# Moving one transposing load of x from SyncE's DMA queue to ScalarE's in a fused linear-attention kernel

## The chip, the cores and the metric

The kernel runs on one core of a Trainium2 chip. The metric is the device time of one execution in microseconds (us); a time that is quoted for a kernel is the median of its runs. A profile comes from one execution, and its span runs from the first to the last instruction that it recorded.

## The reference

Two linear-attention blocks, A and B, read the same x (A_x; B_x is not used), and a per-token gate mixes their outputs. S = 2048 tokens, D = 640 features, H = 32 heads of 20 features, everything in bf16.

```
def block(x, wqkv, wo):                       # once with A's weights, once with B's
    q, k, v = split(x @ wqkv)                 # 32 heads of 20
    phi = lambda t: where(t > 0, t + 1, exp(t)) + 1e-6
    pq, pk = phi(q), phi(k)
    kv = einsum("bhsd,bhse->bhde", pk, v)
    z  = einsum("bhsd->bhd", pk)
    num = einsum("bhqd,bhde->bhqe", pq, kv)
    den = einsum("bhqd,bhd->bhq", pq, z)[..., None] + 1e-6
    return (num / den).reshape(B, S, D) @ wo
g = sigmoid((x * gate_w).sum(-1, keepdims=True))
out = g * block(x, A_wqkv, A_wo) + (1 - g) * block(x, B_wqkv, B_wo)
```

## The kernel before

The tokens are cut into 16 tiles of 128 (NT). The work comes in four stages, one after the other on TensorE.

**Stage k.** For every token tile t and for X = A, B, `k_unit(X, t)` multiplies the tile of x^T by the k part of the weights. There are five steps (`k_step`, over NC = 5 chunks of 128 features); each is a 128x512 and a 128x128 matmul (129 columns for B, whose last column holds the gate), at lines 502 and 503. ScalarE takes the exponential (line 535) and VectorE finishes phi (lines 538 and 546). For tiles 0 and 1 the order is written out by hand: A for both tiles, chunk by chunk, then B for both tiles. From tile 2 on it is tile by tile, A and then B. So tile 2 is 20 matmuls, tile 3 the next 20, and so on.

**Stage g.** `g_unit` sums phi(k)^T x over all tokens (lines 632 and 633), with `q_unit` (line 755) between. **Then** `kv_unit` (673), `wp_unit` (709, 710) and the denominators (838) build one 640x640 matrix W' for each block, and **the last stage** (`o_mm`, line 925) multiplies phi(q) by W' and writes the output.

**Loads.** The matmuls of stage k need x transposed (buffer XT, features on partitions). For tiles 0 and 1, x is loaded as it stands (into XN) and TensorE transposes it against an identity (`x_tp`, line 449), after which VectorE copies it to XT (line 464). For tiles 2 to 15 the DMA transposes while it loads: `xt_dma(t0, t1)` issues one transposing DMA for tiles t0 to t1 - 1. Before the change, all of these come from SyncE's queue (called SP in the profile). SP's loads are issued in the order in which the program lists them:

- x of tile 0, A's k weights chunk 0, x of tile 1, A's k weights chunks 1 to 4 (wkA0 to wkA4)
- B's k weights chunks 0 to 4 (wkB0 to wkB4)
- the seven transposing loads: tile 2, 3, 4, 5, 6 and 7, 8 to 11, 12 to 15 (called xt2, xt3, xt4, xt5, xt6, xt8, xt12 here)
- x of tiles 2 to 15 as it stands, then WQ, WV and WO of both blocks

ScalarE's queue (ACT) issues two small loads at the start: the constants (CST, with the identity) and the gate weights (GW). Then it loads its table with a dummy exponential (line 380), and has nothing more until the first exponentials of stage k.

**Who sets the order.** A small list scheduler (`Sched`) places every operation by estimated costs. TensorE's order is the program's; on the other engines it takes what is ready first. While loads are being listed, each load is tied behind the one before it on the same queue (`o.behind = chain.get(q)`). A dependency between engines, or on a DMA, becomes a semaphore wait ahead of the waiting instruction, and what follows on that engine stands behind it. `after` adds such dependencies by hand. All DMAs are issued at line 349.

Of the kernel before, what the change touches and what calls it, by code (L numbers as in the profile page):

```python
# [6 lines left out]
ACT = mybir.ActivationFunctionType  # L7
# [252 lines left out]
def body(nc, A_x, A_wqkv, A_wo, B_x, B_wqkv, B_wo, gate_w, out, log=None):  # L260
# [84 lines left out]
    def dma(q, name, dst, src, nbytes, ins=(), outs=(), after=(), issue=450.0, transpose=False, prio=None):  # L345
        def fn(e):
            d = dst() if callable(dst) else dst
            with nc.allow_non_contiguous_dma(reason="layout"):
                return e.dma_start(d, src() if callable(src) else src, transpose=transpose)  # L349

        o = op(q, fn, 0.0, ins, outs, after, prio=prio, name=name, dma=(issue, nbytes, 95.0 if transpose else 330.0))
        if loading:
            o.behind = chain.get(q)
            chain[q] = o
        return o
# [14 lines left out]
    bxn = [Buf("xn%d" % t) for t in range(NT)]  # L370
    bxt = [Buf("xt%d" % t) for t in range(NT)]
# [15 lines left out]
    def ld_wk(q, X, c, after=()):  # L387
        dma(q, "wk%s%d" % (X, c), WK[X][:, c, 0:D], wqkv[X][128 * c : 128 * c + 128, D : 2 * D], 163840, outs=[bwk[X, c]], after=after)

    def xt_dma(t0, t1):  # L390
        dma(
            "SP",
            "xt%d" % t0,
            XT[:, :, 128 * t0 : 128 * t1],
            x[128 * t0 : 128 * t1, :],
            (t1 - t0) * 163840,
            outs=bxt[t0:t1],
            issue=(t1 - t0) * 850.0,
            transpose=True,
        )  # L400

    def w3(X, k):
# [8 lines left out]
        ld_wk("SP", "A", c)  # L411
    for c in range(NC):
        ld_wk("SP", "B", c)
    for t0, t1 in ((2, 3), (3, 4), (4, 5), (5, 6), (6, 8), (8, 12), (12, 16)):
        xt_dma(t0, t1)
    dma("SP", "xr", XN[:, 2:NT, 0:D], x[256:S, :].rearrange("(t p) d -> p t d", p=128), 14 * 163840, outs=bxn[2:])
    for X in XS:
# [655 lines left out]
def bass_gated_mix__linear_attn_block__linear_attn_block__prompt_kernel(nc, *args):  # L1073
    body(nc, *args)
# [28 lines left out]
```

## Time and profile before

| | |
|---|---|
| three runs | 189.91, 190.32, 190.47 us; median 190.32 |
| profiled execution | 190.32 us; its span is 189.0 us |
| granted TensorE clock | 1.000 over the span |
| TensorE matmul (PE) | 184.9 us busy, 98% of the span |
| VectorE (DVE), ScalarE (ACT) | 128.6 us (68%), 95.9 us (51%) |
| DMA | 19.42 MB |

How to read the profile: PE is TensorE's matmul and PEld its weight load, which overlaps the matmuls before it. SPq and ACTq are what the sequencers of SyncE and ScalarE spend on issuing DMAs. A DMA is issued at one time and lands later; "us to landing" is the time between, counted from the start of the issue. The chain of waits is followed back from the last instruction, at each step to what released it. A weight load that starts right behind the previous one shows that TensorE waited for nothing there.

### The profile page before, as it was taken

What the parts mean: (1) busy time and instruction counts of PE and PEld (TensorE: products, weight loads), DVE (VectorE), ACT (ScalarE), POOL (GpSimd) and SP (SyncE); (2) the same over time, 40 slices, a digit from 0 to 9 for tenths busy, and PEclk for the clock granted to TensorE, in tenths of its full rate; (3) what the DMA queues carried; (4) which work ended last, traced back from release to release, by engine and by line L of the source; (5) the groups of instructions that cost most, each with busy time, mean ns of one, the idle gap of its engine ahead of it and who ended that gap; (6) DMA issues with size and microseconds to landing.
All of it is one profiled execution on the core that took longest, in us unless ns stands there. A gap on an engine that the chain in (4) does not pass through costs nothing.

```text
span 189.0 us, 3188 instructions
## 1 busy us (share of the span) xinstructions
PE 184.9 (98%) x1246; PEld 108.3 (57%) x1270; DVE 128.6 (68%) x252; ACT 95.9 (51%) x172; POOL 0.3 (0%) x6
## 2 busy tenths in 40 slices
PE   8999999999999999999999999999999999999995
PEld 3555555555565656656557556655666655555552
DVE  2389888888833556477787698888996962765600
ACT  3255565656554545544584777877626495100012
POOL 0000000000000000000000000000000000000000
PEclk9999999999999999999999999999999999999999
DMA  6999999996014011012000006340011055133322
GB/s 194 283 157 141 242 393 365 356 222 139 3 43 106 0 38 35 0 35 30 8 16 18 3 0 147 104 104 5 0 40 30 17 142 129 38 137 107 136 75 69
DMA packets 29469, 19.42 MB, mean 103 GB/s; under 512 B 17390, under 2 KB 29198, under 8 KB 29454
## 3 DMA queue, kind: packets, MB, share of 16 engines
q1 hardware_dynamic: 29300, 19.17, 39.4%
q8 instruction: 10, 0.16, 0.4%
q10 hardware_dynamic: 154, 0.05, 0.1%
q14 instruction: 5, 0.04, 0.1%
HBM read 9.95 MB, written 2.64 MB: 67 GB/s over the span
## 4 chain that ended last, share of the span: by engine, by line
PE 96%; DMA 2%; issue 1%; SPq 0%; DVE 0%; DVEq 0%
PE ps L925 23%; PE ps L755 22%; PE ps L632 18%; PE ps L502 18%; PE ps L503 5%; PE ps L633 5%; DMA XN<-in_A_x_dram 2%; PE ps L673 2%; PE ps L709 1%; SPq L349 0%; PE ps L449 0%; PE ps L710 0%; PE ps L838 0%; DVE TSB L969 0%; PE ps L483 0%
## 5 line engine op out<-in xcount | busy, mean ns | idle before, releaser
L502 PE MATMUL ps<-WKW,XT 128*128 128x512 bf16 x154 | 43.6, 384 | 0.1
L772 ACT ACTIVATE EK<-ps 128x512 bf16<-128x512 f32 x40 | 23.9, 599 | 31.3 <-PE ps L755 30.1
L503 PE MATMUL ps<-WKW,XT 128*128 128x128 bf16 (+1 forms) x160 | 35.3, 221 | 0.3
L535 ACT ACTIVATE EK<-ps 128x640 bf16<-128x640 f32 x32 | 22.3, 703 | 12.8 <-PE ps L503 8.6
L502 PEld LDWEIGHTS ps<-WKW,XT 128*128 128x128 bf16 x160 | 15.8, 99 | 19.1 <-DVE XT L464 0.6
L755 PE MATMUL ps<-XT,WQA 128*128 128x512 bf16 x96 | 24.0, 379 | 0.1
L755 PE MATMUL ps<-XT,WQB 128*128 128x512 bf16 x95 | 23.3, 379 | 0.4 <-issue 0.2
L632 PE MATMUL ps<-XN,PKB 128*128 128x512 bf16 x80 | 23.5, 379 | 0.0
L782 DVE TENSOR_SCALAR EK<-EK 128x512 bf16<-128x512 bf16 x40 | 11.6, 290 | 17.5 <-ACT EK L772 17.4
L632 PE MATMUL ps<-XN,PKA 128*128 128x512 bf16 x78 | 23.1, 379 | 0.1
L633 PE MATMUL ps<-XN,PKA 128*128 128x129 bf16 x80 | 17.6, 220 | 0.1
L633 PE MATMUL ps<-XN,PKB 128*128 128x129 bf16 x80 | 17.6, 220 | 0.0
L925 PE MATMUL ps<-WPA,EX 128*128 128x128 bf16 (+1 forms) x117 | 17.0, 297 | 0.2
L925 PE MATMUL ps<-WPB,PKA 128*128 128x128 bf16 (+1 forms) x117 | 16.1, 297 | 0.2
L503 PEld LDWEIGHTS ps<-WKW,XT 128*128 128x128 bf16 x160 | 15.8, 99 | 0.0
L755 PEld LDWEIGHTS ps<-XT,WQB 128*128 128x128 bf16 x100 | 10.9, 118 | 8.5 <-issue 0.2
L755 PEld LDWEIGHTS ps<-XT,WQA 128*128 128x128 bf16 x100 | 10.6, 117 | 8.1
L538 DVE TENSOR_SCALAR EK<-EK 128x640 bf16<-128x640 bf16 x32 | 10.4, 325 | 7.0 <-ACT EK L535 7.0
L632 PEld LDWEIGHTS ps<-XN,PKA 128*128 128x128 bf16 x80 | 9.4, 117 | 7.9
L632 PEld LDWEIGHTS ps<-XN,PKB 128*128 128x128 bf16 x80 | 9.4, 117 | 7.8
L971 ACT ACTIVATE TSB<-ps 128x640 bf16<-128x640 f32 (+1 forms) x3 | 2.0, 668 | 23.2 <-PE ps L925 23.2
L546 DVE SCALAR_TENSOR_TENSOR PKA<-ps,EK 128x640 bf16<-128x640 f32 x16 | 13.2, 825 | 0.6
(78 smaller groups left out, 233.1 us busy)
## 6 DMA issues: line engine op xcount, KB each, us to landing
out_dram<-TSB SPq DMA_DIRECT2D x15, 160.0 KB, 1.8
XN<-in_A_x_dram SPq DMA_DIRECT2D x1, 2240.0 KB, 8.8
WKW<-in_A_wqkv_dram SPq DMA_DIRECT2D x5, 160.0 KB, 3.4
WKW<-in_B_wqkv_dram SPq DMA_DIRECT2D x5, 160.0 KB, 4.1
WQA<-in_A_wqkv_dram SPq DMA_DIRECT2D x1, 800.0 KB, 10.5
WQB<-in_B_wqkv_dram SPq DMA_DIRECT2D x1, 800.0 KB, 11.7
WVA<-in_A_wqkv_dram SPq DMA_DIRECT2D x1, 800.0 KB, 12.8
WVB<-in_B_wqkv_dram SPq DMA_DIRECT2D x1, 800.0 KB, 14.1
```

The costliest lines, as they stand in the source:

```text
L502: e.matmul(a[:, 0:512], l, WK[X][:, c, 0:512], start=(c == 0), stop=(c == NC - 1))
L503: return e.matmul(a[:, 512:w], l, WK[X][:, c, 512:w], start=(c == 0), stop=(c == NC - 1))
L535: op("ACT", lambda e: e.activation(EK[:, ek.slot, :], psw(ps, D), ACT.Exp), act_cost(D), ins=[ps] + first, outs=[ek], name="ke")
L538: lambda e: e.tensor_scalar(EK[:, ek.slot, :], EK[:, ek.slot, :], 1.0, EPS, op0=ALU.min, op1=ALU.add),
L546: lambda e: e.scalar_tensor_tensor(PKt[X][:, t, :], psw(ps, D), 0.0, EK[:, ek.slot, :], op0=ALU.max, op1=ALU.add),
L632: e.matmul(a[:, 0:512], l, XN[:, t, 0:512], start=(t == 0), stop=(t == NT - 1))
L633: return e.matmul(a[:, 512 : D + 1], l, XN[:, t, 512 : D + 1], start=(t == 0), stop=(t == NT - 1))
L673: r = e.matmul(PS[0:GR, ps.slot, GR * i : GR * i + GR], WV[X][:, c, lo : lo + GR], gv[:, c, :, lo // 5 : lo // 5 + 24], start=(c == 0), st ...
L755: r = e.matmul(PS[:, ps.slot, :], WQ[X][:, c, g::5], XT[:, c, 512 * b : 512 * b + 512], start=(c == 0), stop=(c == NC - 1),)
L772: lambda e: e.activation(EQ[:, eq.slot, :], PS[:, ps.slot, :], ACT.Exp),
L782: lambda e: e.tensor_scalar(EQ[:, eq.slot, :], EQ[:, eq.slot, :], 1.0, EPS, op0=ALU.min, op1=ALU.add),
L925: r = e.matmul(a[:, l0 - lo : h0 - lo], PQ[X, b][:, g, 128 * (t % 4) : 128 * (t % 4) + 128], WP[X][:, g, l0:h0], start=(X == first and g = ...
```

## The change

`xt_dma` takes a queue and a list of things to wait for. The load of tile 2 (xt2) goes to ScalarE's queue and waits until x of tile 1 has landed (`bxn[1].writers` is that DMA). The load of tile 3 (xt3) stays on SP and waits until xt2 has landed (`bxt[2].writers` is the DMA of xt2). The other five transposing loads, and all loads behind them on SP, follow xt3 as before.

```diff
-    def xt_dma(t0, t1):
+    def xt_dma(t0, t1, q="SP", after=()):
         dma(
-            "SP",
+            q,
             "xt%d" % t0,
             XT[:, :, 128 * t0 : 128 * t1],
             x[128 * t0 : 128 * t1, :],
...
             issue=(t1 - t0) * 850.0,
             transpose=True,
+            after=after,
         )
...
-    for t0, t1 in ((2, 3), (3, 4), (4, 5), (5, 6), (6, 8), (8, 12), (12, 16)):
+    xt_dma(2, 3, "ACT", bxn[1].writers)
+    xt_dma(3, 4, "SP", bxt[2].writers)
+    for t0, t1 in ( (4, 5), (5, 6), (6, 8), (8, 12), (12, 16)):
         xt_dma(t0, t1)
```

The order of the instructions on TensorE, VectorE and GpSimd is the same in both programs. On ScalarE, xt2 stands between the dummy exponential and the first exponential of stage k. On SP the first transposing load, now xt3, carries the wait for xt2.

## The prediction

> **What bounds the kernel now.** First the engines on the page, then the chain of waits on the page.
>
> ```profile
> PE 184.9 (98%) x1246; PEld 108.3 (57%) x1270; DVE 128.6 (68%) x252; ACT 95.9 (51%) x172; POOL 0.3 (0%) x6
> PE 96%; DMA 2%; issue 1%; SPq 0%; DVE 0%; DVEq 0%
> ```
>
> TensorE is busy for 98% of the span, and 96% of the chain is TensorE. The only DMA on the chain is one load of x. The chain of waits of the first 14 us shows it:
>
> ```profile
> 0.91 3.55 DMA XN<-in_A_x_dram
> 4.51 0.72 PE ps L449 x5
> ```
>
> It is x of tile 1, issued at 0.91 and landed at 0.91 + 3.55 = 4.46. From there on the chain is TensorE. So a change to the loads can take time from the kernel only where TensorE waits for a load, and can add time only by making it wait; a wait early in stage k moves all that follows by its own length, since TensorE has no idle time later to absorb it.
>
> Next the timeline of TensorE around the first matmuls that use a transposing load. These are weight loads; columns are start, duration, engine, line.
>
> ```profile
> 10.84 0.10 PEld L502 LDWEIGHTS ps<-WKW,XT 128*128 128x128 bf16 x1
> ...
> 13.56 0.10 PEld L502 LDWEIGHTS ps<-WKW,XT 128*128 128x128 bf16 x1
> ```
>
> Tile 2 starts at 10.84, tile 3 at 13.56, so one tile takes 2.72 us, and the weight loads come at their usual step of 0.27 us: no wait at either. Tile 4 is due at 13.56 + 2.72 = 16.28, tile 5 at 19.00, tile 6 at 21.72, tile 8 at 27.16, tile 12 at 38.04.
>
> Then SP's timeline and, by narrow windows of the DMA view, the time from issue to landing of each transposing load (the last column). xt2, xt3, xt4, xt5 in that order, then the one for GSA, which the kernel issues much later, at 58.04, from SBUF and beside little else:
>
> ```profile
> 5.66 14.46 SPq L349 DMA_TRANSPOSE XT<-in_A_x_dram  x7
> ```
>
> ```profile
> XT<-in_A_x_dram SPq DMA_TRANSPOSE x1, 4.5
> ```
>
> ```profile
> XT<-in_A_x_dram SPq DMA_TRANSPOSE x1, 3.8
> ```
>
> ```profile
> XT<-in_A_x_dram SPq DMA_TRANSPOSE x1, 3.9
> ```
>
> ```profile
> XT<-in_A_x_dram SPq DMA_TRANSPOSE x1, 4.0
> ```
>
> ```profile
> GSA<-WKW SPq DMA_TRANSPOSE x1, 2.6
> ```
>
> xt2 lands at 5.66 + 4.5 = 10.2, which is 0.7 ahead of its use. xt3 (issued at 7.01) lands at 10.8, 2.7 ahead of its use. xt4 (8.31) lands at 12.2 and xt5 (9.63) at 13.6, with 4.1 and 5.4 to spare.
>
> **Part 1: xt2 is issued from ScalarE after x of tile 1 has landed.** That is 4.46 plus a hop of about 0.1, so about 4.55: 1.1 us earlier than before. Nobody waited for xt2, so an earlier landing gains nothing by itself: 0.0 us. Cost on ScalarE: one transposing issue, 1.30 us on SP (the median of the seven in the view of the DMA line, from 1.26 to 4.76). ScalarE's timeline has nothing between 2.68 and 8.09, so it is hidden; even 3.5 us would end at 8.05. If that cover were gone, the exponentials of tile 0 would be late, and with them VectorE's last operation on it (ends at 10.01), which frees the PSUM for tile 2: that has 0.8 us to spare as well.
>
> **Part 2: xt2 now runs beside the weight loads.** Before, it stood behind wkB4 in the same queue. How two queues share the DMA engines is to be seen once in this trace, from 1.6 to 2.2 us, where ScalarE's constants (q10) meet SP's loads (q1). The DMA view of that window gives packets, MB and share:
>
> ```profile
> q1 hardware_dynamic: 142, 0.16, 77.1%
> q10 hardware_dynamic: 147, 0.05, 31.1%
> ```
>
> They alternate packet for packet, though q1's packets are 1280 B. A pair takes 0.6 us / (145 / 16 engines) = 0.066 us on one engine. xt2 is 640 packets of 256 B, 40 on each engine. Those constants were issued at 0.12 and had no packet before 1.5, so I let xt2's begin 1.5 us after issue, at 6.1. From 6.1 to 8.8 the trace before moves these:
>
> ```profile
> DMA packets 952, 0.75 MB, mean 277 GB/s; under 512 B 441, under 2 KB 952, under 8 KB 952
> ```
>
> 952 - 441 = 511 of the 1280 B packets are left for weights at 6.1, or 32 per engine. Shared one for one, 32 pairs take 2.1 us, or up to 2.7 if the weights keep their old pace, and the last 8 of xt2 0.2 us (25 ns each): the last packet leaves at 8.4 to 9.0. xt2's last packet before left at about 9.2 and it landed at 10.2, so 1.0 us is for the landing. xt2 lands between 9.4 and 10.0; I take 9.7. So of the 1.1 us that the issue moves forward, about half is lost by sharing. Bounds from the nearest rows: 3.8 from issue to landing (xt3's row) gives 8.4, and 2.6 (the GSA row) gives 7.2; at the other end the DMA engines have the same bytes to move as before, so 10.2 as before.
>
> The weights pay for the sharing: up to 8 pairs' worth of small packets for each wkB, 8 x 0.025 = 0.2 us more with each, at most 5 x 0.2 = 1.0 for wkB4. Before, the five land 4.1, 4.1, 4.1, 4.0, 4.0 after issues at 3.28, 3.75, 4.23, 4.71 and 5.18, which is 0.7, 0.8, 0.9, 1.0 and 1.1 ahead of the weight loads that need them (8.11, 8.66, 9.20, 9.75, 10.29). wkB0's packets are mostly gone by 6.1. So 0.0 us; from 0 to 0.3 if each packet costs half as much again beside the other queue.
>
> [...]
>
> **Part 3: xt3 waits until xt2 has landed, and all SP loads behind it wait too.** Before, SP issued xt3 at 7.01 whatever had landed. Now it is issued at 9.7 + 0.05, and with 3.9 from issue to landing (rows 3.8, 3.9, 4.0) it lands at 13.65, where TensorE wants it at 13.56. That is a wait of 0.1 us on the path. The rows bound it: xt2 at 8.4 and 3.8 for xt3 give 12.2, no wait; xt2 at 10.2 and 4.5 for xt3 (the row of the load that stood behind other traffic) give 14.7, a wait of 1.1 us.
>
> [...]
>
> Behind xt3 everything on SP moves by 9.75 - 7.01 = 2.75 us, at most 3.2. xt4: 12.2 + 2.75 = 14.9, wanted at 16.28. xt5: 16.3, wanted at 19.0. xt6 (issued 10.95, 4.0): 17.7, wanted at 21.7. xt8 (12.54, 7.3): 22.6, wanted at 27.2. xt12 (17.34, 4.9): 25.0, wanted at 38.0. The plain x of tiles 2 to 15 (issued 20.16, 8.8): 31.7, wanted in stage g at about 48.9. WQA lands at 34, wanted at 50.0. SP's next issue behind the loads waits until 51.6 for VectorE. All of it is hidden, with 1.4 us at xt4 as the least, so only xt3 counts.
>
> **The sum.** The profiled execution took 190.32 us, 1.32 outside its span of 189.0; it equals the median of the three runs. 190.32 + 0.0 (part 1) + 0.0 (part 2) + 0.1 (part 3) = 190.4 us. With xt2's own spread (9.4 to 10.0) the wait is 0 to 0.4, so this case runs from 190.2 to 190.8, the lower end by the runs' own spread.
>
> **The rivals.** (a) *Slower: the wait for xt2 is paid in full at tile 3.* If xt2 lands as late as before, xt3 lands at 10.2 + 0.05 + 3.9 = 14.15 and TensorE waits 0.6 us; if xt3 takes 4.5, 1.1 us. Time: 190.9 to 191.4, say 191.0. It decides from xt2's landing at about 10.2 (or xt3's at 14.1) on. For it: the packets alternate one for one, the DMA engines are full between 4 and 9 us, and a transposing issue from ScalarE is not to be seen in this trace. Against: xt2 still starts 1.1 us earlier. (b) *Faster: xt2 was late in executions that were not profiled.* It has only 0.7 us to spare, and the runs differ by 0.56. An early xt2 would then bring them to the lowest of the three or a little under, 189.6. Against: in the profiled execution, which took the median time, nothing waited for it. (c) *Nothing is to be seen:* xt2 finishes quickly, lands by 9.3, all is hidden: 190.3. For it: 4.5 from issue, as before, gives 9.05.
>
> **How the numbers follow.** What can be told from no change is about 0.3%, 0.57 us: from 189.75 to 190.89. The forecast gets 0.37 and (c) 0.22; both lie within, 0.59 together. (a) gets 0.33, since only some 0.5 us separates my value from its threshold; (b) 0.08. The range goes from 189.9 to 191.2: it leaves out (b) and the upper end of (a), 0.18 together.
>
> **What would show it.** In the profile after: ScalarE's sequencer issues xt2 between 4.5 and 5.0, and SP's next transposing issue starts at about 9.7 where before it was 7.0. Tile 2's first weight load still comes at 10.8, tile 3's between 13.55 and 14.0, and every later step of TensorE is moved by that same difference. I am wrong if xt2 lands before 8.5 or after 10.2, if weight loads of B are late ahead of 10.8, if tile 4 or a later one waits, or if TensorE reaches tile 2 at another time than before, because then something other than the queue order counts.

## The result, and the profile after

The changed kernel takes 191.43 us (median of its runs) against 190.24 us before; the ratio is 1.0052, with a 95% interval from 1.0029 to 1.0075. It is slower by about 1 us. Its first profiled execution ran with a granted TensorE clock of 0.194 and took 955.92 us; it is left out here, and the profile shown comes from a later execution of the same kernel, in the last set below (191.00 us, span 189.7, clock 1.000).

The same two lines of the page as before:

```profile
PE 186.4 (98%) x1270; PEld 108.2 (57%) x1270; DVE 128.7 (68%) x252; ACT 95.9 (51%) x172; POOL 0.3 (0%) x6
PE 93%; DMA 3%; SPq 2%; issue 0%; DVE 0%; DVEq 0%
```

TensorE is still the bound, but the chain now holds 3% of DMA where it was 2%, and SP's issues. Which DMA that is, the chain of waits of the first 14 us tells:

```profile
4.72 5.71 DMA WKW<-in_B_wqkv_dram
10.43 0.05 issue
10.47 0.39 PE ps L505
```

Before, the chain came through x of tile 1, which landed at 4.46. Now it comes through a load of B's k weights, wkB3: issued at 4.72 as before (4.71), it lands 5.7 us later at 10.43. Before, it took 4.0 and landed at 8.71, ahead of the weight load that needs it (9.75):

```profile
WKW<-in_B_wqkv_dram SPq DMA_DIRECT2D x1, 160.0 KB, 4.0
```

```profile
9.47 0.10 PEld L502 LDWEIGHTS ps<-WKW,XT 128*128 128x128 bf16 x1
9.53 0.10 PEld L503 LDWEIGHTS ps<-WKW,XT 128*128 128x128 bf16 x1
9.75 0.10 PEld L502 LDWEIGHTS ps<-WKW,XT 128*128 128x128 bf16 x1
```

After, TensorE's weight loads show the wait (the bracket gives the idle time of the weight loader and who ended it):

```profile
9.44 0.10 PEld L505 LDWEIGHTS ps<-WKW,XT 128*128 128x128 bf16 x1
9.49 0.10 PEld L506 LDWEIGHTS ps<-WKW,XT 128*128 128x128 bf16 x1
10.47 0.10 PEld L505 LDWEIGHTS ps<-WKW,XT 128*128 128x128 bf16 x1 [0.88 <-DMA WKW<-in_B_wqkv_dram]
...
11.52 0.10 PEld L505 LDWEIGHTS ps<-WKW,XT 128*128 128x128 bf16 x1
```

The step from 9.44 to 10.47 is 1.03 and should have been 0.27, so 0.76 of the 0.88 us is loss. Tile 2 starts at 11.52 instead of 10.84, and tile 3 at 14.24, one undisturbed tile (2.72) later. The whole difference is made by then: 11.52 - 10.84 = 0.68, and this execution took 191.00 against 190.32 us, which is 0.68 more. (The two executions come from different sets, so the match to the last digit is partly luck.)

The moved load itself, in ScalarE's timeline, with its time to landing from the DMA view of that moment; then SP's transposing loads and the landing of the first of them, xt3:

```profile
4.46 1.31 ACTq L349 DMA_TRANSPOSE XT<-in_A_x_dram  x1
```

```profile
XT<-in_A_x_dram ACTq DMA_TRANSPOSE x1, 6.2
```

```profile
10.63 12.29 SPq L349 DMA_TRANSPOSE XT<-in_A_x_dram  x6
```

```profile
XT<-in_A_x_dram SPq DMA_TRANSPOSE x1, 3.0
```

xt2 is issued 1.2 us earlier than before and lands 0.4 us later, at 10.6. xt3 is issued 3.6 us later than before, but alone it takes 3.0 us, lands at 13.6 and is 0.6 ahead of its use.

### The profile page after: what moved, and what is told of

Same layout as the page of the kernel before. It is cut to its first block, busy times and chain, and to the rows that moved or that the text cites. A ratio compares the mean times of both kernels' runs of the same rounds, so it can differ in the third digit from the quotient of the medians.

```text
span 954.6 us, 3184 instructions
## 1 busy us (share of the span) xinstructions
PE 932.1 (98%) x1246; PEld 341.2 (36%) x1270; DVE 131.4 (14%) x252; ACT 98.0 (10%) x172; POOL 0.3 (0%) x6
## 4 chain that ended last, share of the span: by engine, by line
PE 97%; issue 2%; DMA 1%; SPq 0%; DVE 0%; ACT 0%; DVEq 0%
PE ps L928 27%; PE ps L758 27%; PE ps L635 22%; PE ps L505 9%; PE ps L636 6%; PE ps L506 2%; PE ps L676 2%; PE ps L712 2%; DMA WKW<-in_B_wqkv_dram 1%; SPq L349 0%; PE ps L713 0%; PE ps L841 0%; DVE TSB L965 0%; ACT WKW L726 0%; ACT WKW L644 0%
## 5 line engine op out<-in xcount | busy, mean ns | idle before, releaser
L758 PE MATMUL ps<-XT,WQB 128*128 128x512 bf16 x95 | 132.2, 1707 | 4.7 <-issue 3.7
L758 PE MATMUL ps<-XT,WQA 128*128 128x512 bf16 x96 | 134.5, 1706 | 1.9 <-issue 1.9
L635 PE MATMUL ps<-XN,PKB 128*128 128x512 bf16 x80 | 131.8, 1705 | 0.0
L635 PE MATMUL ps<-XN,PKA 128*128 128x512 bf16 x78 | 128.5, 1702 | 1.9 <-issue 1.9
L505 PE MATMUL ps<-WKW,XT 128*128 128x512 bf16 x154 | 106.7, 783 | 0.0
L928 PE MATMUL ps<-WPA,EX 128*128 128x128 bf16 (+1 forms) x117 | 97.9, 1196 | 2.8 <-issue 1.9
L928 PE MATMUL ps<-WPB,PKA 128*128 128x128 bf16 (+1 forms) x117 | 96.4, 1194 | 2.8 <-DVE TSB L965 1.9
L636 PE MATMUL ps<-XN,PKA 128*128 128x129 bf16 x80 | 57.6, 720 | 1.9 <-issue 1.9
L636 PE MATMUL ps<-XN,PKB 128*128 128x129 bf16 x80 | 57.9, 724 | 0.0
L635 PEld LDWEIGHTS ps<-XN,PKA 128*128 128x128 bf16 x80 | 26.2, 328 | 79.2 <-issue 79.2
L636 PEld LDWEIGHTS ps<-XN,PKA 128*128 128x128 bf16 x80 | 25.9, 324 | 17.6 <-issue 15.0
## 6 DMA issues: line engine op xcount, KB each, us to landing
WQB<-in_B_wqkv_dram SPq DMA_DIRECT2D x1, 800.0 KB, 13.6
```

The costliest lines, as they stand in the source:

```text
L505: e.matmul(a[:, 0:512], l, WK[X][:, c, 0:512], start=(c == 0), stop=(c == NC - 1))
L635: e.matmul(a[:, 0:512], l, XN[:, t, 0:512], start=(t == 0), stop=(t == NT - 1))
L636: return e.matmul(a[:, 512 : D + 1], l, XN[:, t, 512 : D + 1], start=(t == 0), stop=(t == NT - 1))
L758: r = e.matmul(PS[:, ps.slot, :], WQ[X][:, c, g::5], XT[:, c, 512 * b : 512 * b + 512], start=(c == 0), stop=(c == NC - 1),)
L928: r = e.matmul(a[:, l0 - lo : h0 - lo], PQ[X, b][:, g, 128 * (t % 4) : 128 * (t % 4) + 128], WP[X][:, g, l0:h0], start=(X == first and g = ...
```

## The experiments

Six theories were set against each other. **M**: a transposing load whose packets alternate on the DMA engines with those of plain loads from another queue slows both; B's weights come late. **W**: the wait of xt3 for xt2 costs. **B** and **P**: any second queue would do as much, by its bytes (B) or by its 256 B pieces (P). **F** and **Q**: a transposing load ahead of the weights costs by itself (F), or ScalarE's queue does (Q). Ratios are to the kernel before, run on the same chip, with the 95% interval.

**The changed kernel again.** No edit.

> The changed kernel itself, for a profile at full clock over the whole span. Theory M (mixing): the packets of xt2 alternate on each DMA engine with those of wkB1 to wkB4, both get slower than their bytes explain, and TensorE waits about 1.1 us for wkB3 at about 9.7; then 191.2 to 191.6 us, and no wait at tiles 2 or 3. Theory W (the wait of xt3 for xt2): the loss is at tile 3, 0.6 us or more, and the weights of B are on time.

Measured: 191.5 us, 1.0082 (1.0060 to 1.0104). The profiled execution was the quickest of its six, 190.45 us; even in it the weight loads wait for B's weights twice (times in total, number, longest):

```profile
PEld ps L505 <- DMA WKW<-in_B_wqkv_dram: 1.0, 2, 0.7
```

There is no wait at tile 2 or 3, so the place is M's and not W's. M had named wkB3 and 1.1 us; here wkB3 costs 0.2 us, and the longest wait is for wkB4, which lands at 10.42.

**The wait alone.** xt2 goes back to SP, xt3 still waits for it.

```diff
-    xt_dma(2, 3, "ACT", bxn[1].writers)
+    xt_dma(2, 3)
     xt_dma(3, 4, "SP", bxt[2].writers)
```

> xt2 stays on SP where it was; only xt3 waits until xt2 has landed. Theory W: xt2 lands at 10.2, xt3 is issued at 10.25 and takes 3.9, so that TensorE waits 0.6 us at tile 3: 190.8 to 191.0 us. Theory M: nothing runs beside the weights, a transposing load with nothing beside it takes 3.0 us, so xt3 lands at 13.2, ahead of 13.56: 190.1 to 190.4 us, as before.

Measured: 1.0008 (0.9993 to 1.0024), no loss. xt2 lands at 10.1, xt3 is issued at 10.11 and takes this long:

```profile
XT<-in_A_x_dram SPq DMA_TRANSPOSE x1, 2.7
```

It lands at 12.8, ahead of its use. W falls.

**A plain copy in xt2's place on ScalarE's queue.** The kernel before, and in addition:

```diff
+    dma("ACT", "x2", XN[:, 2, 0:D], x[256:384, :], 163840, outs=[bxn[2]], after=bxn[1].writers)
...
-    dma("SP", "xr", XN[:, 2:NT, 0:D], x[256:S, :].rearrange("(t p) d -> p t d", p=128), 14 * 163840, outs=bxn[2:])
+    dma("SP", "xr", XN[:, 3:NT, 0:D], x[384:S, :].rearrange("(t p) d -> p t d", p=128), 13 * 163840, outs=bxn[3:])
```

> The kernel before, with a plain copy of x of tile 2 (the same 160 KB) issued by ScalarE after x of tile 1 has landed, and left out of the later load of x; all transposing loads stay on SP. Theory B (bytes alone: any second queue with 160 KB beside the weights delays them as much): wkB3 is late and TensorE waits about 1 us, 191.2 to 191.4 us. Theory M: plain copies share without loss, the weights come up to 0.5 us later (160 KB at 330 GB/s), which their 0.7 to 1.1 us of slack hides; xt2 lands at 10.6, still in time: 190.1 to 190.5 us.

Measured: 1.0028 (1.0015 to 1.0041). That is a third of what the changed kernel lost on the same chip (1.0082). wkB3 and wkB4 land at 9.47 and 9.93, some 0.8 later than before, and in the profiled execution TensorE waits for neither. So B explains a part and not the whole. M had expected the slack to hide the delay, and it did not hide all of it.

**The transposing load ahead of wkB2, on SP's own queue.** The kernel before, with xt2 moved forward:

```diff
     for c in range(NC):
+        if c == 2:
+            xt_dma(2, 3)
         ld_wk("SP", "B", c)
-    for t0, t1 in ((2, 3), (3, 4), (4, 5), (5, 6), (6, 8), (8, 12), (12, 16)):
+    for t0, t1 in ((3, 4), (4, 5), (5, 6), (6, 8), (8, 12), (12, 16)):
```

> xt2 stays on SP, but ahead of wkB2 instead of behind wkB4; no load waits for another. Theory F (a transposing load ahead of wkB2 to wkB4 delays them by what it takes, on whichever queue): wkB3 lands at about 10.7 as in the changed kernel, 191.2 to 191.5 us. Theory M: in one queue the packets do not alternate, xt2 takes 1.0 us of the engines, wkB2 to wkB4 land 0.8 to 1.3 us later than before and TensorE waits 0 to 0.4 us: 190.2 to 190.7 us.

Measured: 1.0039 (1.0024 to 1.0054), half of the loss. In one queue xt2 takes 3.9 us from issue to landing, not 6.2, and wkB4 lands at 10.1. F is too large. The time, 190.53, lies in M's range, but the kernel before ran at 189.8 on this chip, so it is a loss of 0.7 us where M allowed 0.4. The run does more than change the order of the packets: a transposing issue takes 1.3 us on SP where a plain one takes 0.43, so wkB2 to wkB4 are also issued about 1.4 us later (wkB2 at 5.59 instead of 4.23). How much of the 0.7 us that is, no run separates.

**xt2 from ScalarE, but later.** The changed kernel with another thing to wait for: wkA4 (lands at about 6.6 us), wkA2 (about 5.2) or, in a later set, wkA3 (about 5.7), in place of x of tile 1 (4.5). The queue, the wait of xt3 and all else stay.

```diff
-    xt_dma(2, 3, "ACT", bxn[1].writers)
+    xt_dma(2, 3, "ACT", bwk["A", 4].writers)
```

> The changed kernel, but xt2 waits until wkA4 (about 6.5 us) has landed instead of x of tile 1 (4.5). Its packets came 2.4 us after the issue in the changed kernel, so they start at about 8.9, when the weights' packets are through. Theory M (a transposing load that alternates with plain copies from another queue slows both): wkB4 lands at about 9.2 as before, xt2 at 10.3 to 10.6, TensorE waits 0 to 0.3 us: ratio 1.000 to 1.003. Rival Q (a transposing load from ScalarE's queue, or the wait of xt3 for it, costs whatever it meets): ratio 1.006 to 1.010 like the changed kernel.

> Between the two: xt2 waits until wkA2 (about 5.3 us) has landed, its packets start at about 7.7 and meet only the last third of B's weights. Theory M: the loss grows with the overlap, so it lies between that of the kernel with wkA4 and that of the changed kernel, wkB4 lands at 9.6 to 10.3, ratio 1.002 to 1.006. Rival Q: ratio 1.006 to 1.010.

Measured: wkA4 1.0004 (0.9983 to 1.0026), wkA2 0.9979 (0.9958 to 1.0000). The loss is gone in both, so Q falls: the same load on the same queue, with the same wait behind it, costs nothing that can be measured when it is issued 0.8 to 2.2 us later. With wkA4, xt2 is issued at 6.69 and lands at 10.1, earlier than in the changed kernel, which issued it at 4.46. For wkA2 I had expected a part of the loss, 1.002 to 1.006; that was wrong. Its profiled execution does show a short wait for B's weights (0.5 us in total), but the median pays nothing.

**Two transposing loads from ScalarE.** xt3 follows xt2 there and waits for nothing; xt4 on SP waits for xt3.

```diff
     xt_dma(2, 3, "ACT", bxn[1].writers)
-    xt_dma(3, 4, "SP", bxt[2].writers)
-    for t0, t1 in ( (4, 5), (5, 6), (6, 8), (8, 12), (12, 16)):
+    xt_dma(3, 4, "ACT")
+    xt_dma(4, 5, "SP", bxt[3].writers)
+    for t0, t1 in ((5, 6), (6, 8), (8, 12), (12, 16)):
```

> The changed kernel with xt3 issued by ScalarE as well, right behind xt2, so that xt3 waits for nothing and xt4 on SP waits for xt3. Theory W (the wait of xt3 costs): gone, ratio 1.000 to 1.003. Theory M: the weights meet twice as many transposing packets at their end, wkB4 lands no earlier than in the changed kernel (10.4 to 10.9), ratio 1.006 to 1.013.

Measured: 1.0054 (1.0032 to 1.0075), although xt3's wait is gone. The weight loads wait for B's weights longer than in any other run:

```profile
PEld ps L506 <- DMA WKW<-in_B_wqkv_dram: 1.7, 2, 1.5
```

This is M again and not W. The time at the median is no worse than the changed kernel's on the other chips (1.0052 to 1.0082), and below the 1.006 to 1.013 that M gave for it.

**A plain copy cut into 256 B pieces.** Like the plain copy above, but in the 640 pieces of a transposing load, to a place that a later load overwrites:

```diff
+    dma("ACT", "x2", XN[:, 3:8, 0:128], x[256:384, :].rearrange("p (c f) -> p c f", c=NC), 163840, outs=bxn[3:8], after=bxn[1].writers)
```

> The kernel before, with a plain copy of x of tile 2 added on ScalarE's queue after x of tile 1 has landed, cut into the same 640 pieces of 256 B as a transposing load (to a place that is loaded over later). All transposing loads stay on SP. Rival P (small packets from a second queue are enough): the weights of B come as late as in the changed kernel (wkB4 at 10.4 or later), ratio 1.006 to 1.010. Theory M (it takes the transposing): like the plain copy of 1280 B rows, wkB4 at 9.7 to 10.0, ratio 1.002 to 1.004.

Measured: 1.0013 (0.9996 to 1.0030), where the double transposing load on the same chip gave 1.0054. wkB3 and wkB4 land at 9.5 and 10.2. In this profile x of tile 1 landed early, at 3.7, so TensorE was ahead and did wait for B's weights, 0.7 us in three short waits; the runs as a whole lose 0 to 0.6 us. By the times P falls. By the landings the case is less clear: wkB4 at 10.2 lies between M's 9.7 to 10.0 and P's 10.4 or later, and close to the 10.42 of the changed kernel run again. The DMA view from 7.0 to 8.7 us, first of the changed kernel, then of this one (packets, MB, share of the 16 engines; q1 is SP, q10 ScalarE):

```profile
DMA packets 734, 0.38 MB, mean 226 GB/s; under 512 B 536, under 2 KB 734, under 8 KB 734
q1 hardware_dynamic: 221, 0.25, 67.6%
q10 hardware_dynamic: 513, 0.13, 47.2%
```

```profile
DMA packets 947, 0.58 MB, mean 339 GB/s; under 512 B 607, under 2 KB 947, under 8 KB 947
q1 hardware_dynamic: 470, 0.46, 79.8%
q10 hardware_dynamic: 477, 0.12, 31.1%
```

About as many small packets pass on q10, 513 and 477, but beside transposing ones SP moves 0.25 MB, beside plain ones 0.46. The totals agree: 0.38 MB in this stretch in the changed kernel's executions of 191.00 and 190.45 us, 0.54 with the plain copy of 1280 B rows, 0.58 with this one. One packet of q10 takes 0.472 x 16 x 1.7 us / 513 = 25 ns when it transposes and 18 ns when it does not. For q1 the changed kernel gives 0.676 x 27.2 / 221 = 83 ns for a packet. In the kernel with wkA4, the same loads have the engines to themselves from 7.0 to 7.8 us, before xt2's packets begin:

```profile
q1 hardware_dynamic: 252, 0.29, 98.9%
```

That is 0.989 x 16 x 0.8 us / 252 = 50 ns, so in this profile the plain loads' packets take 1.7 times as long. The factor is not a constant. The earlier profile of the changed kernel (190.45 us) has the first line below from 7.0 to 8.7, which is 0.523 x 27.2 / 224 = 64 ns. In the kernel before, the weights alone have the second from 6.2 to 7.0, which is 0.959 x 12.8 / 169 = 73 ns.

```profile
q1 hardware_dynamic: 224, 0.25, 52.3%
```

```profile
q1 hardware_dynamic: 169, 0.19, 95.9%
```

Nor are the plain packets slow from the first mixed one on. In the profile of 191.00 us they cost 0.547 x 12.8 / 135 = 52 ns from 7.0 to 7.8, and 0.780 x 12.8 / 78 = 128 ns from 7.8 to 8.6:

```profile
q1 hardware_dynamic: 135, 0.15, 54.7%
```

```profile
q1 hardware_dynamic: 78, 0.09, 78.0%
```

With wkA2, in the last set, xt2's packets pass beside the last of the weights from 7.8 to 8.6, and there a packet of q1 costs 0.473 x 12.8 / 125 = 48 ns:

```profile
q10 hardware_dynamic: 415, 0.11, 108.0%
q1 hardware_dynamic: 125, 0.13, 47.3%
```

So the short overlap there does not raise the price of the weights' packets, and in the long one of the changed kernel the price rises after some 0.8 us. Why it rises, no run here shows.

**A last set on one chip**, for the spread between chips and for the 0.9979:

> The changed kernel once more, on the chip of the next two, so that the three share the runs of the kernel before. Theory M: ratio 1.004 to 1.010, TensorE waits for wkB3 or wkB4. If chips alone made the difference between the earlier sets: ratio under 1.003.

> The changed kernel with xt2 waiting for wkA2, once more, to see whether it is faster than the kernel before or the same. Nothing that TensorE waited for before is taken away, so theory M says the same: ratio 0.999 to 1.002. If the earlier 0.9979 was real: 0.996 to 0.999, and xt2 or the weights would have to land earlier than before in the profile.

> xt2 waits until wkA3 (about 5.7 us) has landed, so its packets start at about 8.1. Theory M: the weights are nearly through, wkB4 lands at 9.2 to 9.9, ratio 0.999 to 1.003. Rival Q (the queue or the wait of xt3 costs): 1.004 to 1.010 like the changed kernel.

Measured: the changed kernel 1.0054 (1.0031 to 1.0077), with wkA2 1.0000 (0.9980 to 1.0020), with wkA3 1.0011 (0.9988 to 1.0034). The 0.9979 was not repeated. The later issue brings the kernel back to the time before and not below it; none of the kernels beats the kernel before. In this set's profile with wkA2 the weights land as before (wkB4 at 9.2), TensorE waits for no weights, and xt2, issued at 5.52, lands at 9.8.

## Why the prediction was right or wrong

**What bounds the kernel: right.** TensorE and nothing else; a wait early in stage k goes one to one into the end (0.68 us at tile 2, 0.68 us in the execution).

**Part 1: right.** ScalarE issues xt2 at 4.46 in 1.31 us, inside its idle time, and nothing is gained by it.

**Part 2: the step that failed.** "The weights pay for the sharing ... So 0.0 us; from 0 to 0.3 if each packet costs half as much again beside the other queue." The sum took a packet's price from the one stretch of the trace where two queues meet, 1.6 to 2.2 us, but there both are plain copies. A transposing load was put in with the 25 ns a packet that it takes on its own, and its neighbours with theirs. The 25 ns is in the trace before, from 8.8 to 10.2 us, where all packets are under 512 B: 1.178 x 16 x 1.4 us / 1057.

```profile
q1 hardware_dynamic: 1057, 0.25, 117.8%
```

Measured, wkB3 lands 1.7 us later than before (10.43 against 8.71), more than all of xt2's own engine time of 1.0 us (640 x 25 ns / 16), and TensorE loses 0.76 us in the profile. In the other profile wkB3 lands 0.6 us later than before and wkB4 1.2 us. The plain copies show what the argument is good for: with 1280 B or 256 B pieces the loss is 0.28% and 0.13%, 0.2 to 0.5 us. The rest is lost only where a transposing load runs beside the weights (1.0052 to 1.0082 for the changed kernel), and it goes away when xt2 is issued 0.8 us or more later (0.9979 to 1.0011).

A second flaw lies in the same step: the slack of 0.7 to 1.1 us was read from one execution. In the profiles TensorE reached its full pace at times that differ by 1 us (below), so in some executions the weights have less slack than that: in the changed kernel's execution of 190.45 us, TensorE is ready for B's first weights at 7.59 instead of 8.11, so that all five were due 0.5 us earlier. That this is why the two plain copies and the forward xt2 cost something, though the profiles of the 1280 B copy and of the forward xt2 show no wait for weights, is argued and not shown.

**xt2's landing: outside.** 9.4 to 10.0 was expected, with 10.2 as the latest; it was 10.6, so the issue from a second queue, 1.2 us earlier, brought no earlier landing. The limit "the same bytes to move as before" assumed that the engines' throughput does not depend on the mix. From 7.0 to 8.7 us they moved 0.38 MB in the changed kernel, and 0.54 and 0.58 in the kernels with the plain copies.

**Part 3: the wait was sized too dear.** Rows 3.8 to 4.0 for issue to landing came from loads that stood one behind the other; alone the load takes 2.7 to 3.0. So xt3 was in time even though xt2 came later than thought, and the wait alone gave 1.0008, with 1 inside its interval. The loads behind it on SP were hidden, as worked out.

**The rivals.** Rival (a) had about the right time, 190.9 to 191.4, for a wrong reason: its price was to be paid at tile 3, and it was paid at wkB3, before tile 2 begins. The section on what would show it had named this case: "if weight loads of B are late ahead of 10.8". The time lies above the range because its upper end was built from Part 3 alone. Rival (b) did not happen, nor (c).

## What to carry to other kernels

A load that nobody waited for was issued 1.2 us earlier here and gained nothing, but wkB3, which TensorE needs, landed 1.7 us later beside it; look at the slack of every transfer in flight beside a load, not only at its own. A price per packet holds for the stretch it was read from: in the stretches shown a weight packet cost 50 to 73 ns with no other queue beside it, and 64 and 83 ns on average in the changed kernel, 128 in a part of it. If a transposing load must go on another queue, hold it back until the plain loads that are urgent are nearly through; here that cost nothing that was measured (0.9979 to 1.0011), and it landed at 10.1 (wkA4) and 9.8 (wkA2, last set), against 10.6 with the early issue.

## What the runs showed of the hardware

A transposing load of one tile (160 KB) from HBM took 2.7 to 3.0 us from issue to landing when no packet moved at its issue (xt3 in the kernel with the wait alone and in the changed kernel), 3.8 to 4.0 in a row of its kind (xt3 to xt5 before), and 6.0 and 6.2 in the two profiles of the changed kernel, where its packets ran beside plain loads of another queue (513 and 221 packets from 7.0 to 8.7 us in the profile of 191.00 us). Issued from the same queue 0.8 to 2.2 us later, it took 3.4 to 5.1.

The step of TensorE's early matmuls falls from about 0.5 to 0.27 us at a moment that differs between the two executions below, while the granted clock in their records is 1.000 over the span. These are the same weight loads, chunk 1 of A for tile 0 and chunk 0 for tile 1, in the profile of the kernel before and in the first profile with wkA2:

```profile
5.02 0.15 PEld L503 LDWEIGHTS ps<-WKW,XT 128*128 128x128 bf16 x1
...
5.55 0.15 PEld L503 LDWEIGHTS ps<-WKW,XT 128*128 128x128 bf16 x1
```

```profile
4.90 0.10 PEld L506 LDWEIGHTS ps<-WKW,XT 128*128 128x128 bf16 x1
5.12 0.10 PEld L505 LDWEIGHTS ps<-WKW,XT 128*128 128x128 bf16 x1
5.17 0.10 PEld L506 LDWEIGHTS ps<-WKW,XT 128*128 128x128 bf16 x1
```

The step is 0.53 in the first and 0.27 in the second. The matmuls do the same: in the chain of waits of the kernel before, a 128x512 one takes twice as long at 5.22 as at 6.21.

```profile
5.22 0.43 PE ps L502
...
6.21 0.22 PE ps L502
```

In these two profiles the full pace began at about 6.2 and about 5.0 us; what sets the moment, no run here shows. The runs of the kernel before spread over as much, 189.56 to 190.67 but for three of them.
